# 1/rms of three images spread by rounded products, and the second gathers of the first chunk behind a clearing on GpSimd

## The chip, the core and the metric

The kernel runs on one core of a Trainium2 chip. A core has five engines with an instruction queue each: TensorE (PE; its weight loads are shown apart as PEld), VectorE (DVE), ScalarE (ACT), GpSimd (POOL) and SyncE (SP), which here issues most DMAs. The metric is the device time of one execution in microseconds; the kernel before takes 865.17 us (median of three runs, 863.83 to 868.22).

## The reference

The program computes an attention block with talking heads and hands its output to a gated feed-forward block.

```python
def _attn_ref(q, k, v, w_pre, w_post):          # batch 4, 12 heads, 448 tokens, head width 64
    scores = scale * np.matmul(q, k.transpose(0, 1, 3, 2))
    scores = np.einsum('bhij,hg->bgij', scores, w_pre)      # mixes the heads
    attn = np.exp(scores - np.max(scores, axis=-1, keepdims=True))
    attn = attn / (np.sum(attn, axis=-1, keepdims=True) + 1e-09)
    attn = np.einsum('bhij,hg->bgij', attn, w_post)         # mixes the heads again
    return np.matmul(attn, v)

def _moe_ref(x, w_gate, w_val, w_out, rms_g):   # 1792 tokens, 768 -> 1536 -> 768
    rms = np.sqrt(np.mean(x * x, axis=-1, keepdims=True) + 1e-06)
    xn = x / rms * rms_g
    g = xn @ w_gate
    silu = g * (1.0 / (1.0 + np.exp(-g)))
    return silu * (xn @ w_val) @ w_out
```

## The kernel before

The order of all work is written out by hand; nothing is scheduled. The program has two parts. "Image" means one of the four batch entries, with 448 tokens each.

**Part A, attention** (`part_a`, L417). The rows of the score matrices are cut into 16 chunks of up to 120, four an image, and each chunk into five or six steps. For each head pair a product q·k (`qk_mm`, L134) goes to PSUM; ACT and DVE copy it to a tile `st` (`qk_evac`, L146), and DMAs gather the rows of all heads into a tile `r` (L173), so that the heads of one row lie on neighbouring partitions. A step then mixes the heads (`premix`, tile `sp`, L182), takes the row maximum on DVE (L189) and the exponential on ACT (L196), scales the second mixing weights on POOL (L208), mixes again (`postmix`, tile `pm`, L223), and later multiplies by v (L267). Three tiles `r` take turns. They are cleared at the start, because the gathers leave some rows out: `r0` by DVE (L424), `r1` and `r2` by POOL (L425, L436).

For the first chunk each head's gather is in two: the columns of the first three steps at once (L173), the others put on a list `held` and issued after the last product of the chunk (L434). Of the 13 on the list five go to POOL's queue and eight to SP's. SP's gathers reuse eight completion semaphores in turn, with ACT's: a gather waits until the one that used the semaphore last has landed.

Beside this POOL adds the two halves of the attention output `xt` (L290), squares and sums them (L297 to L305), and SP stores them in DRAM.

**Part B, feed-forward** (`part_b`, L737). x is multiplied by the norm's weight and split into a rounded part and a rest (ACT L577, DVE L578), and each product is made of three rounded ones (L600 to L602, L608 to L610). The products of image 0 with the first weight column (`both`, called from `extra`) are laid between the last steps of part A. 1/rms of a token is put behind the product: it stands as a 112x4 tile `y` and has to be spread over all 128 partitions as `ry`. For that POOL makes a diagonal matrix times y (`diagonals`, tile `d`, L358; called in the last steps of part A, once for each of images 0 to 2), and PE multiplies it by a matrix of ones (`spread`, tile `psy`, L368). `first_row` (L791) begins with the spreads of images 0, 1 and 2, in this order, and then goes on with the products of images 1, 2 and 3. Image 3 comes later and has its diagonal made by DVE (`last_rms`, L827).

Engines take their instructions in order. So what stands behind a spread on PE waits until its diagonal is there.

Of the kernel before, what the change touches and what calls it, by code (L numbers as in the profile page):

```python
# [7 lines left out]
F32 = mybir.dt.float32  # L8
F32R = mybir.dt.float32r
# [3 lines left out]
ALU = mybir.AluOpType  # L13
# [3 lines left out]
B, H, S, D = 4, 12, 448, 64  # L17
# [21 lines left out]
JC, JP = 4, 112  # L39
# [6 lines left out]
def attention_moe(ctx: ExitStack, tc, q, k, v, wpre, wpost, mask, ident, wgv, wo, rms_g, out):  # L46
    nc = tc.nc
    NCHUNK = B * NC

    def pool(stack, name, bufs=1, **kw):  # L50
        return stack.enter_context(tc.tile_pool(name=name, bufs=bufs, reuse_waits="tile", **kw))
# [8 lines left out]
    ones = const.tile([128, 128], F32, name="ones")  # L60
# [31 lines left out]
    def setup():  # L92
        nc.vector.tensor_scalar(we, we, D ** -0.5, None, ALU.mult)
        nc.vector.memset(wk_pre, 0.0)
        for i, (o, w) in enumerate(((wk_pre[:, :HR], we), (wk, wp))):
            m = msk[:, i].unsqueeze(1).to_broadcast([128, H, RH])
            o = o.rearrange("p (h r) -> p h r", r=RH)
            nc.vector.tensor_tensor(o, w.unsqueeze(2).to_broadcast([128, H, RH]), m, ALU.mult)
# [7 lines left out]
    def load_q(n, hp, many=3, eng=nc.gpsimd):  # L106
        b, c = divmod(n, NC)
        if not hp:
            qt[n] = pq.tile([128, H // 2, 128], F32, name=f"q{n}", tag="q", bufs=2)
        hp = slice(hp, hp + many)  # L110
        eng.dma_start(qt[n][:, hp], q[b, :, c, hp])
# [9 lines left out]
    r_all = [(pr, pr, pq)[i].tile([128, 2 * KT, S], F32, name=f"r{i}", tag=f"r{i}", bufs=1) for i in range(3)]  # L121
# [160 lines left out]
    ry, sq, sums, xv, d = ({} for _ in range(5))  # L282
# [69 lines left out]
        ]  # L352
        return ops + 3 * step

    def diagonals(b, eng=nc.gpsimd):
        y = xv[b]
        d[b] = b_pools["dd" if b < B - 1 else "t2"].tile([128, S], F32, name="d", tag=f"d{b}" if b < B - 1 else "t", bufs=1 if b < B - 1 else 8)
        eng.tensor_tensor(  # L358
            d[b][:JP].rearrange("p (c i) -> p c i", c=JC),
            eye.unsqueeze(1).to_broadcast([JP, JC, JP]),  # L360
            y.unsqueeze(2).to_broadcast([JP, JC, JP]),
            ALU.mult,
        )

    def spread(b):

        ps = b_pools["ps0" if b == B - 1 else "ps_p"].tile([128, S], F32, name="psy", tag="p")
        nc.tensor.matmul(ps, ones[:JP], d.pop(b)[:JP], start=True, stop=True)  # L368
        ry[b] = (b_pools["wr"] if b == B - 1 else b_pools["t2"]).tile([128, S], F32, name=f"ry{b}", tag=f"ry{b}", bufs=1)
        nc.scalar.activation(ry[b], ps, AF.Copy)  # L370


    steps = [(n, p) for n in range(NCHUNK) for p in range(PAIRS[n % NC])]
    T = len(steps)
# [7 lines left out]
    for blk, ns in enumerate(BLOCKS):  # L382
        lo = first[ns[-1] + 1] + 1
        hi = first[ns[-1] + (3 if ns[-1] < 13 else 2)] + 1
        units = [(blk, i, part) for i in range(H // 2) for part in ((0, 1) if len(ns) > 1 else (None,))]
        for i, a in enumerate(units):
            t = lo + i * (hi - lo) // len(units)
# [7 lines left out]
    for n in range(NCHUNK):  # L395
        b, c = divmod(n, NC)
# [20 lines left out]
    def part_a(extra):  # L417
        for j in range(H // 4):
            load_q(0, 2 * j, 2, nc.scalar)
            load_k(0, 2 * j)  # L420
            load_k(0, 2 * j + 1)
        load_consts()
        load_q(1, 0, 6, nc.sync)
        nc.vector.memset(r_all[0], 0.0)  # L424
        nc.gpsimd.memset(r_all[1], 0.0)  # L425
        nc.vector.memset(ones, 1.0)
        for hp in range(H // 2):
            alone(qk_mm(0, hp))
            for j in range(2):
                qk_evac(0, hp, j)  # L430
            if hp == 4:
                setup()
        for i, args in enumerate(held):
            (nc.gpsimd if i % 5 in (1, 3) else nc.sync).dma_start(*args)  # L434
        load_q(2, 0)
        nc.gpsimd.memset(r_all[2], 0.0)  # L436
        load_q(2, 3)
        for hp in range(AHEAD):
            alone(qk_mm(1, hp))
            for j in range(2):  # L440
                qk_evac(1, hp, j)
        busy, = banks(ps_v, "busy", 1)
        for _ in range(4):
            nc.tensor.matmul(busy[:, :S], ones, kt[0, 0], start=True, stop=True)
        nc.sync.dma_start(g_sb, rms_g)
        nc.sync.dma_start(eye, ident)
        done = []
        for t in range(T + 24):
            def back(lag):
                return steps[t - lag] if 0 <= t - lag < T else None  # L450

            if t == first[NCHUNK - 1]:
                qk_ctx.close()
                start_b()
            for f, *a in jobs_at[t]:
                f(*a)
            while stored:
                x_store(*stored.pop(0))
            done = [(k, i // 2) for k, i, part in (av_at[t - 1] if t else []) if i % 2 and part != 0]
            sp = premix(*back(0)) if back(0) else []  # L460
            if qk_at[t]:
                qk = qk_mm(*qk_at[t][0])
                if any(f is sq_all and not a[1] for f, *a in last_at[t - 1]):
                    qk.reverse()
                order = sp[:1] + qk[1:] + sp[1:] + qk[:1]
            else:
                order = sp
            for x in order:
                for y in x:
                    y()  # L470
            for a in done:
                av_copy(*a)
            if back(0):
                rowmax(*back(0))
                expo(*back(0))
            if back(1):
                postmix(*back(1))
            for a in av_at[t]:
                av_mm(*a)
            for a in qk_at[t][:1]:  # L480
                for j in range(2):
                    qk_evac(*a, j)
            if back(1):
                for v_ in range(2):
                    evac_a(*back(1), v_)
            if back(0) and t >= T - 2:
                norm(*back(0))
            for op in sum_ops[: 1 if t < first[NCHUNK - 2] else 2 if t <= T else 4]:
                op()
                sum_ops.pop(0)  # L490
            if back(0) and t < T - 2:
                norm(*back(0))
            for a in qk_at[t][1:]:
                alone(qk_mm(*a))
                for j in range(2):
                    qk_evac(*a, j)
            for f, *a in last_at[t]:
                f(*a)
            for a in done:
                x_sum(*a)  # L500
            extra(t - T, bool(done))
            if t >= T + 4 and not done and not stored and not sum_ops and not any(av_at[t:]):
                break


    b_pools = {}
# [43 lines left out]
    def t_tile(name, tag="t", bufs=8):  # L550
        return b_pools["t2"].tile([128, S], F32, name=name, tag=tag, bufs=bufs)
# [117 lines left out]
    def start_b():  # L669
        b_pools["t2"] = pool(late, "t2", side="right")  # L670
        b_pools["x"] = pool(late, "xa", side="right")
        b_pools["w2a"] = pool(late, "w2a", side="right")
        b_pools["dd"] = pool(dd_ctx, "dd", side="right")
        b_pools["ps0"] = pool(late, "ps0", 2, space=PSUM, side="right")
        w[0] = [b_pools["w2a"].tile([128, FT, 128], F32R, name=f"w{n}", tag=f"w{n}") for n in "hl"]

        def w_load(p):
            raws["w", p] = t_tile("wf")[:, :384]
            nc.sync.dma_start(raws["w", p], wf[p // 2][:, (p % 2) * 384 : (p % 2) * 384 + 384])

        def w_split(p):
            hi, lo = (t[:, 3 * p : 3 * p + 3] for t in w[0])
            f = raws.pop(("w", p)).rearrange("p (a f) -> p a f", f=128)
            nc.scalar.activation(hi, f, AF.Copy)
            nc.gpsimd.tensor_tensor(lo, f, hi.bitcast(F32), ALU.subtract)

        def x_item(b, kk):
            todo.append([(x_load, b, kk), (x_split, b, kk, nc.vector), 0.7, 0, 0.9])

        for kk, p in ((0, 0), (None, 2), (1, 1), (None, 3)):  # L690
            if kk is not None:
                x_item(0, kk)
            todo.append([(w_load, p), (w_split, p), 0.5, 1.0, 0])
        for b in range(B - 1):
            for kk in range(0 if b else 2, KT):
                x_item(b, kk)
# [40 lines left out]
    def part_b(ps_p, raw_ctx):  # L737
# [83 lines left out]
        def last_rms(stage):  # L821
            if stage == 0:
                ps = b_pools["ps0"].tile([128, S], F32, name="pss", tag="p")
                column_sums(ps, 3)
                for op in rsqrt(ps[:JP, :JC], 3, const):
                    op()
                diagonals(3, nc.vector)  # L827
            else:
                spread(3)
                swiglu(3, 0, *first_ps[3])  # L830
# [164 lines left out]
```

## Time and profile before

| | |
|---|---|
| median of three runs | 865.17 us (863.83 to 868.22) |
| the profiled execution | 866.41 us, of which the profile's span is 864.6 us |
| PE busy | 827.3 us, 96% of the span |
| POOL busy | 437.6 us, 51% |
| DVE busy, ACT busy | 600.4 us, 69%; 390.4 us, 45% |
| chain that ended last, by engine | PE 90%, DMA 3%, issue 3%, POOL 2%, DVE 1% |

The chain is followed back from the last instruction, at each step to what released it. Part A ends at about 360 us of the span. Shares over the whole span say little of the two places that the change touches: the first 45 us, where gathers are late, and the stretch from 343 to 363 us, where part A passes into part B.

### The profile page before, as it was taken

To read this page: it belongs to the slowest core of one execution; us is meant where nothing else is said; L and a number is where in the kernel's file an instruction comes from. 1 tells how busy PE (TensorE), PEld (TensorE's weight loads), DVE (VectorE), ACT (ScalarE), POOL (GpSimd) and SP (SyncE) were. 2 spreads that over 40 slices of the span, in tenths; PEclk is the share of its full clock that TensorE was granted. 3 is DMA by queue.
4 is the path that set the end of the run, shared out by engine and by line. 5 is a ranking of instruction groups with operands and counts; after the bars stand their busy time and mean duration, and the time that the engine had idled before them with its cause. 6 is when DMAs were issued, how large, how long until landed. Compare 5 with 4: busy or idle time off the path is not lost.

```text
span 864.6 us, 26550 instructions
## 1 busy us (share of the span) xinstructions
PE 827.3 (96%) x10900; PEld 710.8 (82%) x10900; DVE 600.4 (69%) x985; ACT 390.4 (45%) x869; POOL 437.6 (51%) x537
## 2 busy tenths in 40 slices
PE   7899999998899898999999999999999999999998
PEld 2556777777678686799999999999999999999997
DVE  5676787887677666778655858576668359978461
ACT  3677777777677676732211222222121235554310
POOL 7233455554555347935634646365356369573100
PEclk9999999999999999999999999999999999999999
DMA  7777678667756653744634535535354246664541
GB/s 203 202 229 206 202 226 237 213 196 220 223 156 178 184 165 111 231 155 118 215 100 153 139 119 154 179 98 170 105 180 138 64 134 195 201 189 134 170 129 64
DMA packets 77547, 144.53 MB, mean 167 GB/s; under 512 B 10495, under 2 KB 66845, under 8 KB 77427
## 3 DMA queue, kind: packets, MB, share of 16 engines
q1 hardware_dynamic: 72814, 129.19, 49.0%
q0 software_dynamic: 3648, 11.31, 4.8%
q10 hardware_dynamic: 965, 2.34, 0.8%
q8 instruction: 86, 1.41, 0.7%
q14 instruction: 34, 0.28, 0.1%
HBM read 72.03 MB, written 31.21 MB: 119 GB/s over the span
## 4 chain that ended last, share of the span: by engine, by line
PE 90%; DMA 3%; issue 3%; POOL 2%; DVE 1%; ACT 0%; ACTq 0%; SPq 0%; POOLq 0%; DVEq 0%
PE pm L223 9%; PE qk L134 8%; PE sp L182 7%; PE av L267 7%; PE pg L608 6%; PE pg L609 6%; PE pv L609 6%; PE pg L610 6%; PE pv L610 6%; PE pv L608 6%; PE po L610 6%; PE po L609 6%; PE po L608 6%; DMA r<-st 3%; POOL d L358 0%
## 5 line engine op out<-in xcount | busy, mean ns | idle before, releaser
L182 PE MATMUL sp<-r,wk_pre 64*64 64x448 f32 x720 | 162.7, 539 | 4.4 <-DMA r<-st 2.0
L134 PE MATMUL qk<-k,q 64*64 64x448 f32 x768 | 154.6, 560 | 5.9 <-DMA q<-in_q 4.1
L196 ACT ACTIVATE e<-sp,nm 128x448 f32<-128x448 f32 x180 | 114.4, 638 | 88.4 <-DVE nm L189 86.2
L223 PEld LDWEIGHTS pm<-wn,e 60*64 60x64 f32 x5152 | 110.1, 134 | 50.9 <-POOL wn L208 21.5
L189 DVE TENSOR_REDUCE nm<-sp 128x1 f32<-128x448 f32 x180 | 111.5, 622 | 56.2 <-PE sp L182 25.3
L208 POOL TENSOR_SCALAR wn<-wk,rp 128x60 f32<-128x60 f32 x180 | 55.8, 322 | 162.4 <-DVE rp L205 143.1
L223 PE MATMUL pm<-wn,e 60*64 60x60 f32 x5152 | 109.5, 220 | 18.0 <-issue 14.9
L267 PE MATMUL av<-at_all,v 64*64 64x240 f32 (+4 forms) x1728 | 95.1, 319 | 3.6 <-issue 3.6
L608 PE MATMUL pg<-x,wh 128*128 128x448 f32 x264 | 96.8, 367 | 0.0
L609 PE MATMUL pv<-x,wh 128*128 128x448 f32 x264 | 96.4, 365 | 0.0
L608 PE MATMUL pv<-x,wh 128*128 128x448 f32 x264 | 96.4, 365 | 0.0
L610 PE MATMUL pg<-x,wl 128*128 128x448 f32 x264 | 96.4, 365 | 0.0
L610 PE MATMUL pv<-x,wl 128*128 128x448 f32 x264 | 96.4, 365 | 0.0
L609 PE MATMUL pg<-x,wh 128*128 128x448 f32 x264 | 96.4, 365 | 0.0
L595 DVE TENSOR_TENSOR x<-hraw,x 128x448 fp32r<-128x448 f32 x84 | 91.6, 1137 | 6.8 <-ACT x L594 6.8
L609 PE MATMUL po<-x,fac 128*128 128x448 f32 x252 | 92.1, 365 | 0.0
L608 PE MATMUL po<-x,fac 128*128 128x448 f32 x252 | 92.0, 365 | 0.0
L610 PE MATMUL po<-x,fac 128*128 128x448 f32 x252 | 92.0, 365 | 0.0
L642 POOL TENSOR_TENSOR sg<-sg,u 128x448 f32<-128x448 f32 x36 | 48.1, 1335 | 83.0 <-DVE u L638 43.5
L637 ACT ACTIVATE sg<-g 128x448 f32<-128x448 f32 x48 | 27.4, 571 | 129.2 <-DVE g L636 118.6
L182 PEld LDWEIGHTS sp<-r,wk_pre 64*64 64x64 f32 x720 | 62.4, 133 | 22.2 <-issue 9.6
L638 DVE TENSOR_TENSOR u<-pv,ry 128x448 f32<-128x448 f32 x48 | 29.9, 623 | 69.1 <-PE pv L610 60.6
(118 smaller groups left out, 1709.9 us busy)
## 6 DMA issues: line engine op xcount, KB each, us to landing
r<-st SPq DMA_DIRECT2D x117, 210.0 KB
hraw<-td SPq DMA_DIRECT2D x84, 224.0 KB
wraw<-in_wgv SPq DMA_DIRECT2D x20, 768.0 KB
td<-keep SPq DMA_DIRECT2D x48, 224.0 KB
wraw<-in_wo SPq DMA_DIRECT2D x12, 768.0 KB
r<-st SPq DMA_DIRECT2D x44, 175.0 KB
v<-in_v SPq DMA_DIRECT2D x24, 256.0 KB
q<-in_q POOLq DMA_DIRECT2D x28, 192.0 KB, 5.1
```

The costliest lines, as they stand in the source:

```text
L134: nc.tensor.matmul(ps[j][m, :S], qt[n][sl, hp, m], kt[n // NC, hp][sl], start=True, stop=True)
L182: nc.tensor.matmul(o, wk_pre[sl], rt[n][sl, 2 * p + v_], start=True, stop=True)
L189: nc.vector.tensor_reduce(t, ps[:, :S], AX.X, ALU.max, negate=True)
L196: nc.scalar.activation(e, ps[:, :S], AF.Exp, bias=nmx.pop((n, p, u)), accum_out=sm[n, p][:, u : u + 1])
L208: nc.gpsimd.tensor_scalar(wn[n, p][:, u], wk, r[:, u : u + 1], 1.0, ALU.mult, ALU.mult)
L223: nc.tensor.matmul(o[:, :, at_], e[u_][sl, j : j + JT], w_, start=True, stop=True)
L267: nc.tensor.matmul(x, vt[b, hp][sl, j, c_], a, start=(c_ == 0), stop=(c_ == JC - 1))
L595: nc.vector.tensor_tensor(lo, raw, hi.bitcast(F32), ALU.subtract)
L608: nc.tensor.matmul(ps, a, xh[:, kk], start=(kk == 0), stop=False)
L609: nc.tensor.matmul(ps, a, xl_[:, kk], start=False, stop=False)
L610: nc.tensor.matmul(ps, a2, xh[:, kk], start=False, stop=(kk == KT - 1))
L642: nc.gpsimd.tensor_tensor(h, sg, u, ALU.mult)
```

## The change

There are three edits.

1. For images 0 to 2, y is split into a rounded part `yh` (a copy on POOL that rounds) and the rest `yl` (a subtraction on POOL). POOL makes one diagonal of each (`dh`, `dl`), and PE makes `psy` of two rounded products, added in PSUM, in place of one plain fp32 product. A rounded copy of the matrix of ones is made once by DVE. Image 3 stays as it was.
2. In the first chunk POOL now loads q of chunk 2 and clears `r2` before it issues its five held gathers, not after. SP's eight stand where they stood.
3. `setup()` (five small DVE instructions that make the mixing weights) comes after the copies of head pair 5, not 4.

```diff
-    def diagonals(b, eng=nc.gpsimd):
-        y = xv[b]
-        d[b] = b_pools["dd" if b < B - 1 else "t2"].tile([128, S], F32, name="d", ...)
+    def diagonal(o, y, eng):
         eng.tensor_tensor(
-            d[b][:JP].rearrange("p (c i) -> p c i", c=JC),
+            o[:JP].rearrange("p (c i) -> p c i", c=JC),
             eye.unsqueeze(1).to_broadcast([JP, JC, JP]),
             y.unsqueeze(2).to_broadcast([JP, JC, JP]),
             ALU.mult,
         )
+    def diagonals(b):
+        y, p_ = xv[b], b_pools["dd"]
+        hi, lo = (p_.tile([JP, JC], F32R, name=f"y{n}{b}", tag=f"y{n}{b}") for n in "hl")
+        nc.gpsimd.tensor_copy(hi, y)
+        nc.gpsimd.tensor_tensor(lo, y, hi.bitcast(F32), ALU.subtract)
+        d[b] = []
+        for n, part in (("h", hi), ("l", lo)):
+            t = p_.tile([128, S], F32R, name=f"d{n}{b}", tag=f"d{n}{b}")
+            diagonal(t, part.bitcast(F32), nc.gpsimd)
+            d[b].append(t)
     def spread(b):
-        nc.tensor.matmul(ps, ones[:JP], d.pop(b)[:JP], start=True, stop=True)
+        if b == B - 1:
+            nc.tensor.matmul(ps, ones[:JP], d.pop(b)[:JP], start=True, stop=True)
+        else:
+            hi, lo = d.pop(b)
+            nc.tensor.matmul(ps, b_pools["ones"][:JP], hi[:JP], start=True, stop=False)
+            nc.tensor.matmul(ps, b_pools["ones"][:JP], lo[:JP], start=False, stop=True)
...
-            if hp == 4:
+            if hp == 5:
                 setup()
+        load_q(2, 0)
+        nc.gpsimd.memset(r_all[2], 0.0)
         for i, args in enumerate(held):
             (nc.gpsimd if i % 5 in (1, 3) else nc.sync).dma_start(*args)
-        load_q(2, 0)
-        nc.gpsimd.memset(r_all[2], 0.0)
         load_q(2, 3)
...
+        b_pools["ones"] = b_pools["dd"].tile([128, 128], F32R, name="ones_r", tag="ones_r")
+        nc.vector.tensor_copy(b_pools["ones"], ones)
```

On POOL, where part A passes into part B, before (y_5261 and y_6950 are the 1/rms of images 1 and 2; `d` are their diagonals):

```order
L290 TENSOR_TENSOR xt_7706<-xt_7706,xt_7707 128x200
L358 TENSOR_TENSOR d<-eye,y_5261 112x448
L297 TENSOR_TENSOR xt_7707<-xt_7706 128x200
L302 TENSOR_TENSOR sum_6957<-xt_7707 128x100
L290 TENSOR_TENSOR xt_7769<-xt_7769,xt_7770 128x200
L358 TENSOR_TENSOR d<-eye,y_6950 112x448
L297 TENSOR_TENSOR xt_7770<-xt_7769 128x200
```

The same place on POOL with the change:

```order
L290 TENSOR_TENSOR xt_7714<-xt_7714,xt_7715 128x200
L366 CAST yh_7774<-y_5261 112x4
L367 TENSOR_TENSOR yl_7775<-y_5261,yh_7774 112x4
L356 TENSOR_TENSOR dh_7778<-eye,yh_7774 112x448
L356 TENSOR_TENSOR dl_7780<-eye,yl_7775 112x448
L297 TENSOR_TENSOR xt_7715<-xt_7714 128x200
L302 TENSOR_TENSOR sum_6957<-xt_7715 128x100
L290 TENSOR_TENSOR xt_7783<-xt_7783,xt_7784 128x200
L366 CAST yh_7843<-y_6950 112x4
L367 TENSOR_TENSOR yl_7844<-y_6950,yh_7843 112x4
L356 TENSOR_TENSOR dh_7847<-eye,yh_7843 112x448
L356 TENSOR_TENSOR dl_7849<-eye,yl_7844 112x448
```

Each diagonal has become four instructions at the same place in the order; nothing else on POOL is moved there, and image 0 goes the same way.

On POOL at the start of the program, before (`r_119`, `r_120` and `r_121` are r0, r1 and r2; L434 are the held gathers, and the L173 behind them those of chunk 1):

```order
L173 DMA r_119<-st 10x6x448 x3
L434 DMA r_119<-st 10x6x448 x4
L434 DMA r_119<-st 5x6x448
L111 DMA q_238<-in_q 128x384
L436 MEMSET r_121 128x5376
L111 DMA q_238<-in_q 128x384
L173 DMA r_120<-st 10x12x448 x4
```

With the change:

```order
L173 DMA r_119<-st 10x6x448 x3
L111 DMA q_225<-in_q 128x384
L447 MEMSET r_121 128x5376
L449 DMA r_119<-st 10x6x448 x4
L449 DMA r_119<-st 5x6x448
L111 DMA q_225<-in_q 128x384
L173 DMA r_120<-st 10x12x448 x4
```

The five held gathers stand behind one load and the clearing; the rest of POOL's order is the same.

## Rows read from the trace of the kernel before

**Rows 1.** The page's first line.

```profile
span 864.6 us, 26550 instructions
```

**Rows 2.** Stretches of 362 to 860 us, summed: busy us of each engine.

```profile
sum 498.00, PE 497.99 PEld 460.80 DVE 337.61 ACT 142.71 POOL 247.76; mean PE 124.50 PEld 115.20 DVE 84.40 ACT 35.68 POOL 61.94
```

**Rows 3.** Chain that ended last, 343 to 363 us, shares of that stretch.

```profile
by line: POOL d L358 19.2%; POOL wl L685 17.2%; POOL xt L297 14.6%; POOL xt L290 14.3%; issue 11.3%; POOL sum L305 7.5%; POOL sum L302 5.5%; PE psy L368 5.1%; POOL xt L304 3.9%; POOL wn L208 1.6%; POOLq L290 0.3%; POOLq L685 0.2%
```

**Rows 4.** Timeline of POOL: start us, us, engine, line, operation, tiles, shapes, count.

```profile
357.21 1.31 POOL L358 TENSOR_TENSOR d<-eye,y 112x448 f32<-112x448 f32 x1
...
360.65 1.31 POOL L358 TENSOR_TENSOR d<-eye,y 112x448 f32<-112x448 f32 x1
361.92 0.90 POOL L297 TENSOR_TENSOR xt<-xt 128x200 f32<-128x200 f32 x1
```

**Rows 5.** Timeline of PE, 359.4 to 362.8 us; idle time before in brackets.

```profile
359.48 0.37 PE L602 MATMUL pv<-x,wl 128*128 128x448 f32 x1
359.69 1.67 PE L368 MATMUL psy<-d,ones 112*128 112x448 f32 x4
362.01 1.02 PE L368 MATMUL psy<-d,ones 112*128 112x448 f32 x2 [0.66 <-POOL d L358]
```

**Rows 6.** Waits of SP's queue, 0 to 60 us: total, times, longest.

```profile
SPq L173 <- DMA r<-st: 6.4, 4, 4.9
```

**Rows 7.** Timeline of ACT, 10 to 17 us.

```profile
10.74 1.71 ACTq L173 DMA_DIRECT2D r<-st  x1
...
13.07 0.78 ACTq L173 DMA_DIRECT2D r<-st  x1
```

**Rows 8.** Timeline of SP, from 12.7 us.

```profile
17.64 0.75 SPq L173 DMA_DIRECT2D r<-st  x1
```

**Rows 9.** Timeline of POOL, 7 to 26 us.

```profile
10.31 1.64 POOL L434 DMA_DIRECT2D r<-st  x3
13.33 1.10 POOL L434 DMA_DIRECT2D r<-st  x2 [1.37 <-ACT st L156]
...
15.14 4.60 POOL L436 MEMSET r<- 128x5376 f32 x1
```

**Rows 10.** Chain that ended last, 0 to 62 us, in order of time.

```profile
17.85 3.20 PE busy L444 x8
21.05 0.52 PE sp L182 x2
```

**Rows 11.** Waits, 18 to 62 us.

```profile
PE sp L182 <- DMA r<-st: 1.3, 3, 1.0
```

**Rows 12.** Timeline of POOL, small instructions that need one another.

```profile
327.60 0.20 POOL L346 TENSOR_TENSOR y<-u,y 112x4 f32<-112x4 f32 x1
327.88 0.20 POOL L343 TENSOR_TENSOR u<-y 112x4 f32<-112x4 f32 x1
```

**Rows 13.** Stretches: length, busy us (count) by engine, PEclk, DMA share, GB/s.

```profile
83.40:85.50 2.10, 0.00 (x0) 0.00 (x0) 0.92 (x2) 1.53 (x5) 0.48 (x1) 1.00 0.63 189
...
860.80:863.00 2.20, 0.00 (x0) 0.00 (x0) 0.62 (x1) 0.00 (x0) 0.00 (x0) 1.00 0.28 104
863.00:864.60 1.60, 0.00 (x0) 0.00 (x0) 0.00 (x0) 0.00 (x0) 0.00 (x0) 0.51 0.00 0
```

**Rows 14.** Timeline of PE's weight loads at the start, in groups of four.

```profile
4.12 0.31 PEld L134 LDWEIGHTS qk<-k,q 64*64 64x64 f32 x8 [4.12 <-DMA q<-in_q]
...
8.66 0.24 PEld L134 LDWEIGHTS qk<-k,q 64*64 64x64 f32 x4 [0.51 <-issue]
9.40 0.24 PEld L134 LDWEIGHTS qk<-k,q 64*64 64x64 f32 x4 [0.50 <-issue]
...
10.31 0.14 PEld L134 LDWEIGHTS qk<-k,q 64*64 64x64 f32 x4 [0.23 <-issue]
10.69 0.14 PEld L134 LDWEIGHTS qk<-k,q 64*64 64x64 f32 x4 [0.23 <-issue]
```

**Rows 15.** Timeline of DVE, last steps of part A.

```profile
327.67 1.16 DVE L189 TENSOR_REDUCE nm<-sp 128x1 f32<-128x448 f32 x2 [0.80 <-PE sp L182]
```

More of the change, by code (lines that the diff above doesn't have):

```diff
@@ L353, in rsqrt @@
         return ops + 3 * step
-    def diagonals(b, eng=nc.gpsimd):
-        y = xv[b]
-        d[b] = b_pools["dd" if b < B - 1 else "t2"].tile([128, S], F32, name="d", tag=f"d{b}" if b < B - 1 else "t", bufs=1 if b < B - 1 else 8)
+    def diagonal(o, y, eng):
         eng.tensor_tensor(
-            d[b][:JP].rearrange("p (c i) -> p c i", c=JC),
+            o[:JP].rearrange("p (c i) -> p c i", c=JC),
             eye.unsqueeze(1).to_broadcast([JP, JC, JP]),
@@ L363, in diagonals @@
         )
-    def spread(b):
-        ps = b_pools["ps0" if b == B - 1 else "ps_p"].tile([128, S], F32, name="psy", tag="p")
-        nc.tensor.matmul(ps, ones[:JP], d.pop(b)[:JP], start=True, stop=True)
+    def diagonals(b):
[8 more added lines that the diff above has]
+            d[b].append(t)
+    def spread(b):
+        if b == B - 1:
+            ps = b_pools["ps0"].tile([128, S], F32, name="psy", tag="p")
+            nc.tensor.matmul(ps, ones[:JP], d.pop(b)[:JP], start=True, stop=True)
+        else:
+            ps = b_pools["ps_p"].tile([128, S], F32, name="psy", tag="p")
+            hi, lo = d.pop(b)
+            nc.tensor.matmul(ps, b_pools["ones"][:JP], hi[:JP], start=True, stop=False)
+            nc.tensor.matmul(ps, b_pools["ones"][:JP], lo[:JP], start=False, stop=True)
         ry[b] = (b_pools["wr"] if b == B - 1 else b_pools["t2"]).tile([128, S], F32, name=f"ry{b}", tag=f"ry{b}", bufs=1)
@@ L826, in last_rms @@
                     op()
-                diagonals(3, nc.vector)
+                d[3] = t_tile("d")
+                diagonal(d[3], xv[3], nc.vector)
             else:
```

## The prediction, made before the result was known

> **What bounds the kernel now.** The page and the whole chain come first: the profiled execution took 866.4 us, its span is 864.6 [rows 1], PE carries nine tenths of the chain, so only what makes PE wait, or shortens PE's own work, can count. From 362 to 860 us PE is busy 497.99 of 498.00 us [rows 2]: part B has no slack that could take up a delay, and none that could hide one. What is lost before 362 stays lost.
>
> Second, the chain cut to the stretch where part A passes into part B. There POOL is the chain: its halves' sums, the weights' rests and the diagonals hold it, 19.2% the diagonals alone, PE only 5.1% [rows 3]. POOL's timeline shows it working without a pause; the last diagonal runs from 360.65 and the next instruction starts 1.27 us later [rows 4]. PE's timeline shows the other side: four passes of the first two spreads at 359.69, behind the last product of image 0, then 0.66 us of waiting for the last diagonal, and the third spread at 362.01 [rows 5]. So the end of POOL's last diagonal already sets when PE goes on.
>
> Third, the waits of the start. SP stood 4.9 us before the last gather of chunk 0, for the landing of a gather that ACT issued at 10.74 [rows 6, 7], and issued it at 17.64 [rows 8]. Its semaphore is shared with that one. Five held gathers of POOL are in flight just then (issued 10.31 to 14.4) [rows 9]. But PE hardly follows SP here: `sp` of step 0 starts at 21.05 right behind the filling products that begin at 17.85 [rows 10], and until 62 us PE waits for gathers 1.3 us in all [rows 11].
>
> **The diagonals and the spreads.** Each image gets three more POOL instructions: a copy and a subtraction on 112x4, and a second 112x448 product. Small dependent instructions on such tiles start 0.28 us apart (327.60, 327.88) [rows 12]; a diagonal holds POOL for 1.27 us (three alike, the last from 360.65 to 361.92) [rows 4]. That makes 0.28 + 0.28 + 1.27 = 1.83 us an image, and 5.49 for three, all ahead of or in the last one. POOL has no pause there, and nothing between them is dropped, so the third image's last diagonal is done 5.49 us later: PE's last product of the spreads starts at 362.01 + 5.49 = 367.50.
>
> PE saves little. An fp32 spread is two passes, at most 1.67 / 4 = 0.42 us each [rows 5]; rounded products of the same size start 0.21 apart (359.48 to 359.69) [rows 5]. Of the savings of images 0 and 1 nothing counts, as PE then waits for image 2. There 0.8 us follow the diagonal before; with the change the product of the rounded part runs while POOL makes the second diagonal, and 0.2 us follow. So the delay is 5.49 - 0.6 = 4.9 us. Bounds: POOL may run faster once DVE has no splits left, but hardly below the 0.90 us of a 200-wide product [rows 4], 3 x (0.56 + 0.90) - 0.6 = 3.8; and 5.5 if PE's saving does not come through. I take 4.9, since the three diagonals there are all alike.
>
> The rounding copy on POOL is in no row. From below it may be as cheap as the other small ones (0.20 busy), from above 1.3 us, a 448-wide product; I take 0.28, since what it moves is the same 112x4.
>
> **The clock.** With the change PE has, from 359.7 to 367.7, six products of 0.2 us and nothing else: image 1 is ready at about 358.5 + 2 x 1.83 = 362.1, the rounded part of image 2 at 366.2. So it idles 3.8 us in one piece with other idle time on both sides. [...] Coming back costs time: at the start PE worked from 4.12 on; its groups of four loads stood 0.74 us apart up to 9.40, and 0.38 from 10.31 on [rows 14]. About 5.6 us at half speed lose 2.8 us. I take 2.8, with 0 (the clock holds) as the other end.
>
> [...]
>
> **The start.** The five held gathers of POOL leave the time from 10.3 to 14.4. The load of q needs the first chunk's last product, done at about 11.5 (the twelfth group of four weight loads, at 10.69, belongs to it) [rows 14]; the clearing takes 4.6 us [rows 9], so they are issued from about 16.8 to 19.5, and what follows on POOL stands where it stood, since the same work is only turned round. Held gathers are used in step 3, some 10 us later. The gather that SP waited for shares the DMA engines with fewer others; half of the 4.9 us seems fair, so SP runs 2 to 2.5 us earlier. What PE can get of that is its wait for gathers, 1.3 us [rows 11], less what the five late ones cost again: I take -1.1. Bounds: -2.2, if ACT's issue at 10.74 also falls from 1.71 to 0.78 as the next one [rows 7] and the filling products start 0.9 earlier; +0.5, if the held gathers only crowd the next ones.
>
> **At nothing.** `setup()` moves 0.6 us of DVE work past one copy; nothing reads its tiles before 21.05, and ACT's queue, not DVE, holds the products of chunk 1. If that cover were gone it would cost 0.6. DVE's rounded copy of the ones comes ahead of a row maximum that waits 0.80 us for PE [rows 15], longer than such a copy of 128x128 can take; uncovered, 0.2.
>
> **The sum.** -1.1 + 4.9 + 2.8 = +6.6 us. The profiled execution would go from 866.4 to 873.0. It lies 1.2 us above the median of the runs, so for that I put 865.2 + 6.6 = 871.8.
>
> **Rivals.** *The clock holds.* For: two products of image 2 and the weight loads interrupt the idle time; the 2.1 us at 83.4 did no harm [rows 13]. Against: the end of the trace, where as little was enough. Then -1.1 + 4.9 = +3.8: 869.0.
>
> *The lead of SP is passed on in full, and it comes out not slower.* If the landing at which SP stands comes 4.9 us earlier [rows 6], and all of chunk 0 and 1 moves up with it, -4.9 + 4.9 = 0: 865.2, or 868.0 with the clock's 2.8. It decides from a lead of SP above 2.5 us if PE is bound by gathers. For it: SP issues gathers back to back after 17.64. Against: `sp` starts straight behind products that need no gather [rows 10], and the 1.3 us of waiting [rows 11].
>
> *The second diagonals are hidden.* If PE had something else to do ahead of the third spread, only savings would be left, -1.1 - 0.6 = -1.7: 863.5, faster by 0.2%. Against: the spreads stand in front of all products of image 1, in order, and PE waits there already [rows 5].
>
> *The first rounding copy is slow.* It is a kind of instruction that POOL runs nowhere before. If its first one took as long as a whole diagonal more [rows 4], 1.3 us, the sum is +7.9: 873.1. [...]
>
> **How the numbers follow.** Forecast 0.70 (871.8; its own range 869.5 to 874), clock holds 0.14 (869.0), lead passed on 0.07 (865 to 868), diagonals hidden 0.03 (863.5), slow copy 0.06 (873.1). Runs of this kernel differ by 2 us or so from their median, and about 0.5%, 4.3 us, is what can be told from no change; 869.5 is the border. Slower: 0.70 x 0.9 + 0.14 x 0.4 + 0.06 = 0.75. Faster: a half of the 0.03, and a little of the lead's case: 0.02. Same: 0.23. The range has to hold both clocks and the bounds of the start and of the diagonals; it leaves out most of the two cases below 867: 867.0 to 874.5.
>
> **What would show it.** Right: waits of PE for `dh` and `dl` of some 5 us together between 361 and 367, POOL without a pause up to there, the last `psy` at about 366.4 (367.5 less the start's 1.1), and a dip of the granted clock behind it. Wrong: no wait for the last diagonal; a full clock throughout; an `sp` of step 0 well before 20 us, which would make the start worth more than 1.1; a rounding copy of more than 1 us.

## The result

The changed kernel takes 874.11 us (median of six runs, 870.85 to 876.51), the kernel before 865.04 beside it. The ratio is 1.0117, 95% interval [1.0082, 1.0152], slower by 7 to 13 us. The forecast was 871.8 with a range up to 874.5. On the forecast's own base of 865.17 the ratio gives 875.3: slower as forecast, but by 10.1 us instead of 6.6 and beyond the range. Measured twice more, the changed kernel gave 1.0122 [1.0073, 1.0172] and 1.0088 [1.0053, 1.0123].

The profiled execution took 873.61 us, 7.2 more than that of before. First the transition from part A to part B. POOL's timeline there (start us, us, engine, line, operation, tiles, shapes; image 1, then image 2):

```profile
360.17 0.19 POOL L366 CAST yh<-y 112x4 fp32r<-112x4 f32 x1
360.44 0.53 POOL L367 TENSOR_TENSOR yl<-y,yh 112x4 fp32r<-112x4 f32 x1
360.93 1.37 POOL L356 TENSOR_TENSOR dh<-eye,yh 112x448 fp32r<-112x448 f32 x1
362.26 0.93 POOL L356 TENSOR_TENSOR dl<-eye,yl 112x448 fp32r<-112x448 f32 x1
...
364.65 0.60 POOL L366 CAST yh<-y 112x4 fp32r<-112x4 f32 x1
365.33 0.53 POOL L367 TENSOR_TENSOR yl<-y,yh 112x4 fp32r<-112x4 f32 x1
365.82 1.37 POOL L356 TENSOR_TENSOR dh<-eye,yh 112x448 fp32r<-112x448 f32 x1
367.16 0.93 POOL L356 TENSOR_TENSOR dl<-eye,yl 112x448 fp32r<-112x448 f32 x1
368.05 0.51 POOL L297 TENSOR_TENSOR xt<-xt 128x200 f32<-128x200 f32 x1
```

It answers to [rows 4]. From the copy to the instruction behind the last diagonal POOL now spends 2.99 and 3.40 us where one diagonal took 1.27; the instruction behind image 2's starts at 368.05 and not at 361.92, 6.13 later. PE's timeline, which answers to [rows 5], with the idle time before an instruction in brackets:

```profile
360.10 0.37 PE L381 MATMUL psy<-dh,ones_r 112*128 112x448 f32 x1
360.30 0.37 PE L382 MATMUL psy<-dl,ones_r 112*128 112x448 f32 x1
362.36 0.47 PE L381 MATMUL psy<-dh,ones_r 112*128 112x448 f32 x1 [1.69 <-POOL dh L356]
363.25 0.47 PE L382 MATMUL psy<-dl,ones_r 112*128 112x448 f32 x1 [0.43 <-POOL dl L356]
367.25 0.74 PE L381 MATMUL psy<-dh,ones_r 112*128 112x448 f32 x1 [3.52 <-POOL dh L356]
368.14 0.74 PE L382 MATMUL psy<-dl,ones_r 112*128 112x448 f32 x1
368.68 0.57 PE L613 MATMUL pg<-x,wh 128*128 128x448 f32 x1
369.05 0.57 PE L614 MATMUL pg<-x,wh 128*128 128x448 f32 x1
```

PE waits 5.6 us for diagonals instead of 0.66, and then its products start 0.37 us apart instead of 0.20. Stretches of the same trace (length, PE busy, granted clock, share of the DMA engines, GB/s) show why: behind the wait the clock stands at 0.50 for 2.6 us of work, and then at 1.00:

```profile
368.70:371.30 2.60, 2.60 (x9) 0.50 0.86 347
371.40:372.40 1.00, 1.00 (x7) 1.00 0.08 23
```

Second the start. The chain that ended last, 10 to 35 us, in order of time, which answers to [rows 10]:

```profile
12.17 4.93 DVE we L93
...
22.26 0.52 PE sp L182 x2
...
24.42 9.29 DMA r<-st
...
33.96 1.01 PE sp L182 x2
```

And the three timelines behind it: SP's last gather of chunk 0 and its held ones (the second fence has the held ones before), POOL's clearing, and DVE's `setup()` (its first instruction before in the fence behind it).

```profile
14.79 0.75 SPq L173 DMA_DIRECT2D r<-st  x1
15.64 10.86 SPq L449 DMA_DIRECT2D r<-st  x8
```

```profile
18.49 8.68 SPq L434 DMA_DIRECT2D r<-st  x8
```

```profile
12.47 4.60 POOL L447 MEMSET r<- 128x5376 f32 x1
16.99 2.77 POOL L449 DMA_DIRECT2D r<-st  x5
```

```profile
12.17 4.93 DVE L93 TENSOR_SCALAR we<-we 128x12 f32<-128x12 f32 x1
17.41 1.15 DVE L154 COPY st<-qk 128x448 f32<-128x448 f32 x2
```

```profile
11.50 0.16 DVE L93 TENSOR_SCALAR we<-we 128x12 f32<-128x12 f32 x1
```

SP issues the last gather of chunk 0 at 14.79 instead of 17.64 [rows 8], as it waits 2.4 us there and not 4.9 [rows 6]. But its eight held gathers then take 10.86 us and not 8.68, so that of the 2.85 us some 0.7 are left at their end. And `setup()`'s first instruction, of 12 columns, takes 4.93 us (0.16 before) and ends with POOL's clearing. The copies of q·k behind it are late, and `sp` of step 0 starts at 22.26, not 21.05. Then PE stands 3.11 us in step 3 for a held gather [rows 11: 1.3 us in all], and the clock falls there too (0.50 from 33.42 to 36.83). The first product of part B starts at 347.46, before at 347.02; as the repeats below show, these two executions alone can't tell what the start costs.

### The profile page after: what moved, and what is told of

The parts are those of the page before. It is cut to its first block, busy times and chain, and to the rows that moved or that the text cites. A ratio compares the mean times of both kernels' runs of the same rounds, so it can differ in the third digit from the quotient of the medians.

```text
span 871.8 us, 26564 instructions
## 1 busy us (share of the span) xinstructions
PE 830.7 (95%) x10900; PEld 711.2 (82%) x10900; DVE 602.2 (69%) x986; ACT 390.0 (45%) x869; POOL 442.0 (51%) x546
## 4 chain that ended last, share of the span: by engine, by line
PE 90%; POOL 3%; issue 3%; DMA 2%; DVE 2%; ACT 0%; SPq 0%; POOLq 0%; DVEq 0%; ACTq 0%
PE pm L223 9%; PE qk L134 8%; PE sp L182 8%; PE av L267 7%; PE pg L621 6%; PE pv L621 6%; PE pg L623 6%; PE pv L623 6%; PE pg L622 6%; PE pv L622 6%; PE po L622 6%; PE po L623 6%; PE po L621 6%; DMA r<-st 2%; DVE we L93 1%
## 5 line engine op out<-in xcount | busy, mean ns | idle before, releaser
L223 PE MATMUL pm<-wn,e 60*64 60x60 f32 x5152 | 107.7, 219 | 13.2 <-issue 9.8
```

The source lines that it names most:

```text
L223: nc.tensor.matmul(o[:, :, at_], e[u_][sl, j : j + JT], w_, start=True, stop=True)
```

## The experiments

Executions of one kernel differ by 1.5 to 4.3 us (standard deviation), mostly in part A: with both moves of the start alone the first pv below lies between 342.85 and 352.35 us, the stretch behind it between 53.30 and 53.66. The granted clock of part A differs too; in the three profiles of the changed kernel it is 0.97, 0.92 and 0.97 in the mean of 10 to 62 us. So beside the ratios I read one stretch that holds the transition and nothing of part A: from PE's first product `pv` of part B to the spread of image 3. In the kernel before and the changed kernel it runs between these rows of PE's timeline, 53.14 and 59.75 us:

```profile
347.02 0.36 PE L600 MATMUL pv<-x,wh 128*128 128x448 f32 x1
400.16 0.92 PE L368 MATMUL psy<-d,ones 112*128 112x448 f32 x2
```

```profile
347.46 0.37 PE L613 MATMUL pv<-x,wh 128*128 128x448 f32 x1
407.21 0.92 PE L377 MATMUL psy<-d,ones 112*128 112x448 f32 x2
```

| kernel | ratio to before, 95% interval | first pv, us | stretch, us |
|---|---|---|---|
| before, unchanged, as an experiment | 0.9986 [0.9956, 1.0017] | 348.70 | 53.52 |
| changed, again | 1.0122 and 1.0088 | 351.62, 348.26 | 60.42, 59.65 |
| spreads alone, twice | 1.0083 [1.0047, 1.0119], 1.0113 [1.0068, 1.0158] | 342.55, 346.43 | 60.97, 60.69 |
| both moves of the start alone, three times | 1.0016 [0.9976, 1.0056], 1.0082 [1.0045, 1.0120], 1.0029 [0.9995, 1.0063] | 352.35, 342.85, 348.24 | 53.66, 53.30, 53.63 |
| held gathers alone, twice | 1.0017 [0.9973, 1.0062], 1.0084 [1.0048, 1.0120] | 345.35, 351.48 | 53.79, 53.26 |
| `setup()` alone | 1.0061 [1.0030, 1.0092] | not read | not read |
| changed, `setup()` back | 1.0115 [1.0074, 1.0156] | 347.76 | 59.99 |
| changed, held gathers back | 1.0066 [1.0037, 1.0096] | 343.86 | 60.53 |
| start's moves, clearing cut | 1.0005 [0.9976, 1.0034] | 347.95 | 53.80 |
| spreads alone, waits filled | 1.0040 [1.0012, 1.0069] | 344.51 | 58.17 |
| spreads alone, without the rest | 1.0012 [0.9979, 1.0045] | 343.26 | 55.52 |
| spreads alone, late, twice | 1.0017 [0.9982, 1.0051], 1.0093 [1.0058, 1.0129] | 345.75, 347.54 | 55.95, 55.18 |

### The spreads alone

The kernel before with edit 1 only.

> The rounded spreads alone, the start as before. Theory A (the transition makes nearly all of the loss: POOL's three extra instructions an image, about 5.7 us as the changed kernel's trace has them, and the clock's fall behind them, about 1.5 us, less PE's saving): the kernel is 6 to 7 us longer than before (871 to 872 us, ratio 1.007 to 1.008); the trace shows POOL's last diagonal ending near 367.6, PE waiting for dh of images 1 and 2, and one fall of the granted clock behind it and none near 33 us. Theory B (the start makes the 2 to 3 us by which the medians lie further apart than the two profiled executions do): +6 or less here, and the rest in the run with the start alone. If instead this run alone gives the whole +9 to +10, theory B is wrong and the transition or the clock costs more in other executions than in the profiled one.

It gave 1.0083, theory A's size, and a second time 1.0113. The waits are those of the changed kernel (what waited for what: total, times, longest), and the clock stays at 0.50 for longer, to 368.9:

```profile
PE psy L381 <- POOL dh L356: 5.1, 2, 3.6
```

```profile
363.80:368.80 5.00, 5.00 (x15) 0.50 0.48 188
369.00:370.00 1.00, 1.00 (x7) 1.00 0.91 186
```

One expectation missed: with the start as before the granted clock is 0.97 in the mean of 10 to 62 us, where the profile of before has 1.00. A fall in part A is thus no sign of the start's moves.

> The spreads alone once more (start as before), beside the changed kernel: 1.007 to 1.009 if the start makes the difference of 3 us between the two, 1.010 to 1.012 if the difference so far was chance. From the first pv to PE's last spread of image 3 about 61 us, as the first time (53.5 before).

The repeat, beside the changed kernel (1.0088), came out above it at 1.0113: the 3 us between the two in the first batches were at least partly chance.

### Without the rest

```diff
-        hi, lo = (p_.tile(...) for n in "hl")
-        nc.gpsimd.tensor_tensor(lo, y, hi.bitcast(F32), ALU.subtract)
-        for n, part in (("h", hi), ("l", lo)):
+        hi = p_.tile(...)
+        for n, part in (("h", hi),):
```

> The spreads alone (start as before), with the rounded part only: the rest, its diagonal and its product are left out, so the rows of 1/rms are rounded. POOL then adds only the copy (0.2 to 0.6 us an image in the trace of the spreads alone). If POOL's length ahead of the third spread is what costs, the end of the last diagonal moves by 0.6 to 1.8 us instead of 5.7, PE's wait for it goes from 3.6 to about 1 us, the clock holds, and the stretch from the first pv to the end is 518 to 519.5 us: +0 to +1.5 us over before, 6 to 7 us less than the spreads alone. If the form of the spread (fp32r operands, the new evictions) costs, it stays at 522 or more.

Ratio 1.0012; the stretch is 55.52, 4.8 less than the mean of the seven profiles with the whole edit (60.29). POOL's length is what costs, not the form of the product. The copy took 0.18 to 0.59 us. Wrong was that the clock would hold: PE still waits 3.1 us for one diagonal, and behind it the clock reads 0.50 for 3.3 us (360.7 to 364.0); so the stretch is 2.0 us above the old spreads, and not 0 to 1.5.

```profile
PE psy L380 <- POOL dh L356: 3.1, 1, 3.1
```

### Waits filled

```diff
+            idle = ps_p.tile([128, S], F32, name="idle", tag="p")
+            for b, many in enumerate((0, 8, 15)):
+                for _ in range(many):
+                    nc.tensor.matmul(idle, w[0][0][:, 0], xs[1][0][:, 0], start=True, stop=True)
                 spread(b)
```

> The spreads alone (start as before), and PE fills its waits ahead of the second and third spread with 8 and 15 products of 128x448 into a tile that nothing reads, so that it doesn't stand still. POOL's diagonals take as long as in the spreads alone. Theory (the idle time lets the clock fall, and that costs 1.5 us in the changed kernel and about 3 in the run with the spreads alone): no fall of the granted clock within 10 us of the spreads, products of image 1 at 0.20 us from the first on, and the stretch from the first pv to the end 521.5 to 523 us instead of 525.4. Rival (a clock that falls anyway, or products that delay the spread by as much as the fall costs): 525 or more.

PE's timeline has the fillers in the waits, and the first product of image 1 is followed by the next after 0.21 us:

```profile
357.59 1.81 PE L813 MATMUL idle<-x,wh 128*128 128x448 f32 x8
359.33 0.48 PE L381 MATMUL psy<-dh,ones_r 112*128 112x448 f32 x1
360.23 0.47 PE L382 MATMUL psy<-dl,ones_r 112*128 112x448 f32 x1 [0.41 <-POOL dl L356]
360.53 3.21 PE L813 MATMUL idle<-x,wh 128*128 128x448 f32 x15
363.79 0.47 PE L381 MATMUL psy<-dh,ones_r 112*128 112x448 f32 x1
365.06 0.47 PE L382 MATMUL psy<-dl,ones_r 112*128 112x448 f32 x1 [0.81 <-POOL dl L356]
365.38 0.37 PE L613 MATMUL pg<-x,wh 128*128 128x448 f32 x1
365.59 0.37 PE L614 MATMUL pg<-x,wh 128*128 128x448 f32 x1
```

The clock keeps 1.00 (362 to 368 us), and the stretch is 58.17: 2.1 less than with the spreads as they are, 4.7 more than the mean of eight profiles with the old spreads (53.51). That separates the transition's loss of 6.8 us into 4.7 for POOL and 2.1 for the clock, by one profile with fillers; the seven without lie between 59.65 and 60.97. To the end of the span the stretch did not shrink as expected (525.3 us), because here the last part, from image 3's spread on, took 467.1 us instead of 464.5. The three profiles of the start alone have the same 2.6 us, no other profile has. In the first of them 70 us of the output stage hold 341 products of PE, in the kernel before 347, at a granted clock of 1.00 in both. What makes it is not known; the time of those two kernels contains it.

### Late spreads

```diff
-            for b in range(B - 1):
-                spread(b)
...
+            spread(0)
+            more()
             for kk in range(KT):
                 both(first_ps[1], w[0], xs[1], kk)
+            spread(1)
+            spread(2)
...
```

> The rounded spreads, but those of images 1 and 2 are issued behind the first product group of image 1 instead of ahead of it; the start as before. Theory A says the extra POOL work costs only because the spreads stand ahead of all products of image 1, so that PE waits for the last diagonal: here PE has those products to do, the waits for dh and dl go to nearly 0, the clock does not fall, and the time is that of before or 1 to 2 us less (ratio 0.998 to 1.000). Rival: the evictions of the first products need the spread rows of image 1 (ry) and wait for POOL's diagonal instead, so that PE stalls on full product tiles a few us later: then +2 to +4 us.

Here `both` is the first product group of image 1, and `more()` only takes its PSUM tiles. The waits for diagonals are gone, and others have come in their place: PE reaches a later part of x before ACT and DVE have split it.

```profile
PE pg L613 <- ACT x L590: 1.2, 1, 1.2
PE pg L614 <- DVE x L591: 1.1, 1, 1.1
```

The stretch is 55.95, 2.4 above the old spreads: between theory A and the rival, whose price was right but not its cause.

> The rounded spreads with those of images 1 and 2 behind the first products of image 1, again: the first time it took 0.5 us less than before in the mean (standard error 1.2), though in its profile image 1's next split was late by 2.35 us and the stretch from the first pv to image 3's spread 2.8 us longer. If the order alone made the transition's loss, 0.998 to 1.001; if the split is late in every execution, 1.002 to 1.004.

The second profile has 55.18 with the same two waits (0.9 and 1.3 us). Its ratio of 1.0093 can't be read as the order's, as the section on the start shows. So of the transition's 6.8 us some 4.7, by the mean of these two profiles, lay in the order: a diagonal is dear only where PE has nothing else to do.

### The start's two moves

> The start's two moves alone (held gathers behind the clearing, setup() behind pair 5), the spreads as before. What the changed kernel's trace shows should be here again: setup()'s first DVE instruction takes about as long as POOL's clearing (4.9 us, 0.16 before), `sp` of step 0 starts about 1.2 us later, PE waits about 3 us in step 3, and the granted clock falls there. Theory A (most of that is given back before the transition, 0.4 us left): +0.3 to +1 us, ratio 1.000 to 1.001. Theory B (the start's loss and its falls of the clock vary from one execution to the next, and cost 2 to 4 us in the median): ratio 1.003 to 1.005, with a lower mean granted clock than before in each run. The prediction's own term would be -1.1 us.

> The start's two moves alone, again. If the start costs 2 to 3 us: ratio 1.002 to 1.004, and the first pv at 348 to 352 us in the profile (342.6 to 347.0 with the old start). If it costs nothing in the mean: 0.998 to 1.001, and the first pv among those of the old start. The hold of DVE (4.9 us) and `sp` of step 0 at 22 or later are expected either way.

> The start's two moves alone, a third time (1.0016 and 1.0082 so far). Against the unchanged kernel of the same batch: if the start costs 2 to 3 us in every batch, 0.2 to 0.4% above it; if it costs nothing in the mean, within 0.2% of it.

In all six profiles with both moves (three here, three of the changed kernel) `setup()`'s first instruction takes 4.93 us and `sp` of step 0 starts at 22.2 to 23.4 (20.3 to 22.2 in the eight profiles with the start as before). The wait in step 3 is not always there: PE waited for gathers 0 to 4.3 us between 18 and 62 us, with the old start 0 to 4.5.

### Held gathers alone, and the clearing cut

> The held gathers behind the clearing, setup() where it was (behind pair 4). If setup()'s long DVE instruction comes from running beside POOL's clearing, it is short here (0.16 us, at about 11.5, ahead of the clearing) and `sp` of step 0 starts at about 21 or, if SP's earlier first gathers are worth something, at 20 to 20.5. If the wait of 3 us in step 3 comes from the held gathers alone, it is still there (2.5 to 3.5 us, as PE arrives 1.2 us earlier: up to 4.3) and the clock falls there as well; the time is then within 1 us of the run that has both moves. If the wait came from the delay of the DVE copies, it is gone and the time is that of before or 1 us less.

DVE's `setup()`, PE's first `sp`, and the waits of 18 to 45 us:

```profile
10.55 0.16 DVE L93 TENSOR_SCALAR we<-we 128x12 f32<-128x12 f32 x1
```

```profile
19.66 0.59 PE L182 MATMUL sp<-r,wk_pre 64*64 64x448 f32 x2
```

```profile
PE sp L182 <- DMA r<-st: 4.5, 2, 4.1
```

Ahead of the clearing the instruction is short, and step 0 starts some 1.3 us earlier than in the profile before, 0.7 earlier than in the earliest with the old start. In step 3 PE waits 4.1 us.

> The held gathers behind the clearing alone, again: no hold of DVE, `sp` of step 0 at 19.5 to 21, a wait of 3 to 4 us in step 3 with a fall of the clock. If what SP wins is lost again in step 3, the ratio is 0.999 to 1.002; if the prediction's -1.1 us is to be had once setup() is out of the way, 0.997 to 0.999.

The repeat has no hold either, but `sp` at 21.09, and 6.2 us of waiting for gathers: the gain isn't there each time, the wait was both times.

> The start's two moves as in the changed kernel, spreads as before, but POOL's clearing of the target is cut into 12 memsets of 448 columns each. If setup()'s first DVE instruction can't start or end while one POOL instruction runs, it takes one piece's time here (0.4 to 0.8 us, not 4.9), the DVE copies behind it start at about 13, and `sp` of step 0 starts at 19.5 to 21 instead of 22.2. If DVE is held until POOL leaves the whole row of memsets, it stays at 4.9 and 22.2. The wait in step 3 for a held gather stays in either case (3 to 4 us). Time: within 2 us of before.

The edit, and DVE's and POOL's rows:

```diff
+            for i in range(2 * KT):
+                nc.gpsimd.memset(r_all[2][:, i], 0.0)
-        nc.gpsimd.memset(r_all[2], 0.0)
```

```profile
11.79 0.30 DVE L93 TENSOR_SCALAR we<-we 128x12 f32<-128x12 f32 x1
...
12.13 0.22 DVE L98 TENSOR_TENSOR wk_pre<-we,msk 128x60 f32<-128x60 f32 x1
```

```profile
12.10 5.03 POOL L435 MEMSET r<- 128x448 f32 x12
```

The clearing takes 5.03 us, longer than the 4.60 of the whole one, yet the instruction takes 0.30, and `sp` starts at 20.12. It is recorded 0.3 us ahead of POOL's clearing, as in the changed kernel (12.17 and 12.47), so what holds DVE is the one long POOL instruction; that a piece holds it for its own length isn't shown, as here it ends when the first piece starts. In this run PE waits 5.5 us in step 3, more than in any other.

### Back to before, one move at a time

> The changed kernel itself, once more, beside the experiments of this batch, as executions of one kernel differ by several us here (the start of the run with the spreads alone is that of before, and yet its first product of part B comes 4.5 us earlier). If the loss is the transition's (6.8 and 7.8 us from the first product pv of part B to the end of the span, in the changed kernel and in the run with the spreads alone) plus a start worth 0 to 1, the ratio comes out at 1.008 to 1.010; if the start really costs 2 to 3 us more, at 1.011 to 1.013. In its profile the stretch from the first pv to the end is 524 to 525.5 us (517.6 before), setup()'s first DVE instruction takes 4.9 us again, and PE waits 3 to 4 us for a held gather in step 3.

> The changed kernel, with setup() behind pair 4 again, ahead of the clearing, as in the kernel before. The changed kernel took 1.0117 and 1.0122 of before's time, the spreads alone 1.0083: 3 us more, which only the start can make. Theory L (DVE held by the clearing makes it: step 0 starts 1 to 2.5 us late in the three profiles that have the hold, and PE stands still while the copies are late): setup()'s first instruction takes 0.16 us, `sp` of step 0 starts at 19.5 to 20.5 (22.2 and 23.4 in the changed kernel), and the ratio is 1.008, as with the spreads alone. Theory H (the held gathers, issued late and landing up to 12 us after their issue, make it): PE waits 3 to 5 us in step 3 as in the run with the held gathers moved alone (4.15), and the ratio stays at 1.011 to 1.012.

> The changed kernel, with the held gathers ahead of the clearing again, and setup() behind pair 5. The clearing then starts at about 15, behind setup() (about 12.2), so the hold of DVE should be gone too (0.16 us), and SP stands for the landing of ACT's gather again (`sp` of step 0 at about 21). Theories L and H both expect the ratio of the spreads alone, 1.008. If it stays at 1.011 or more, the 3 us aren't from the start's held gathers at all, but from chance or the later place of setup().

> The changed kernel, for comparison on the same chip as the two runs above and the one below: ratio 1.010 to 1.013 if the two measurements so far hold; step 0 at 22 to 23.5.

With `setup()` back the hold is gone (0.16 us), PE waits 3.6 us in step 3, and the ratio stays at 1.0115, as theory H had it. `sp` starts at 21.12, later than theory L expected. With the held gathers back the ratio is 1.0066, and the first pv comes at 343.86. But the intervals, [1.0074, 1.0156] and [1.0037, 1.0096], overlap, and the spreads alone, with neither move, had 1.0113 beside them: the ratios don't tell the two moves apart.

A mark nearer to the start does. PE's first product with v (tile `av`) starts, in the kernel before, the changed kernel, the held gathers back and the clearing cut, at:

```profile
67.17 0.37 PE L267 MATMUL av<-at_all,v 64*64 64x240 f32 x1
```

```profile
68.92 0.37 PE L267 MATMUL av<-at_all,v 64*64 64x240 f32 x1
```

```profile
67.38 0.37 PE L267 MATMUL av<-at_all,v 64*64 64x240 f32 x1
```

```profile
70.29 0.37 PE L267 MATMUL av<-at_all,v 64*64 64x240 f32 x1
```

In the eight profiles with the start as before it lies between 65.34 and 68.45 (mean 66.8), in the six with both moves between 68.06 and 70.47 (69.3), in the three with the held gathers alone moved between 69.10 and 69.75 (69.4). So the start costs some 2.5 us by then, with a standard error of 0.5. It comes with the held gathers. Taking DVE's hold away, in two ways, gave nothing of it back, and with `setup()` moved alone, in one profile, the product lies among those of the old start.

> setup() behind pair 5 alone, the held gathers ahead of the clearing as before: the clearing starts at about 15, so DVE isn't held (0.16 us), `sp` of step 0 at about 21 as before, and the ratio is that of no change, 0.998 to 1.002. If setup()'s place costs by itself (its 0.6 us ahead of the copies), `sp` comes 0.5 us later.

It missed: 1.0061, where no change was expected. Its profile can't be compared with the others, so what its `setup()` took isn't known; 0.16 us is what it takes at the same place with the held gathers back.

> The kernel before, unchanged, measured like an experiment. If the comparisons are even: ratio 0.998 to 1.002. If a part of the last batch's differences belongs to how the executions of a batch follow one another: 1.003 or more, and then that much has to be allowed for in each of the comparisons here, the changed kernel's too.

In the batch of `setup()` alone, of the second runs of the start's moves, of the held gathers and of the late spreads, all four lay 0.6 to 0.9% above before, and three of them had lain 0.2% above it in an earlier batch. The unchanged kernel shows no such offset in its own batch (0.9986). In that batch it was also the kernel before that ran shorter, 862.6 us in the median against 865.0 to 867.5 in the others. What made the batch differ is open. Between batches a difference under some 0.6% can't be put down to an edit, and the start's cost can't be had from the times more finely than this: 1.4 to 7 us, by the batch, with the 2.6 us of the last part in it. Nor do the ratios of the changed kernel (1.0117, 1.0122, 1.0088) and of the spreads alone (1.0083, 1.0113) show it. The first pv, mean of six profiles with both moves, is 348.5 us, of eight with the start as before 345.7, of the three with the held gathers alone moved 348.2: 2.5 to 2.8 us later, with a scatter of 2 to 3.5 us in each group and so a standard error of some 1.6. That agrees with the 2.5 us at the first `av`, which is the firmer figure.

## Why the prediction fell short

**The diagonals, +4.9.** Right in its mechanism; the size came out by errors that cancel. 5.49 us were forecast for POOL; the last diagonal is done 5.7 us later once the start's 0.44 is taken off. The small instructions were dearer than 0.28 (0.27 to 0.68 from one to the next), the second diagonals cheaper than 1.27 (0.90). PE's waits were to be some 5 us: 5.6. The net cost with the clock held is 4.7. The first rounding copy isn't slow: 0.58 us, so that rival is out.

**The clock, +2.8.** Right that it falls: behind the wait it reads 0.50 for 2.6 us of work in the changed kernel and for 5.0 in the spreads alone, and 1.00 with the waits filled; the five other profiles with the same spreads have stretches as long (59.65 to 60.69 us, filled 58.17). That 3.8 us of idling would be enough was the author's estimate. The runs have a clock at 0.50 behind waits of 3.52 us (changed), 3.6 (spreads alone) and 3.1 (without the rest), and still at 1.00 in the changed kernel's wait of 1.69. The fall cost 2.1 us in the mean (the fillers), 0.7 less than forecast, between about 1.6 in the changed kernel and 2.8 in the spreads alone: over the last wait the clock reads 0.62 in the one and 0.50 in the other, and PE has less or more work at 0.50.

**The start, -1.1.** This is the step that failed. It had three premises.

*SP's lead of 2 to 2.5 us, half of the 4.9 us that SP stood.* It came, 2.85 us, but the 4.9 us were those of one execution: the kernel before, unchanged, issued the same gather at 15.05 in another, with `sp` of step 0 at 20.34.

```profile
15.05 0.75 SPq L173 DMA_DIRECT2D r<-st  x1
```

And SP's list of held gathers used most of the lead up: the eight ended 0.7 us earlier than before.

*Held gathers used late enough ("some 10 us later").* They weren't: the one that PE waited for in step 3 was issued at 24.42 and landed 9.29 us later, and with the held gathers behind the clearing PE waits 2.7 to 5.5 us in step 3 in the four profiles without the hold of DVE, 0 to 3.1 in the six with it, where it comes later; with the old start 0 to 2.3 us. Why the landing takes so long isn't shown. Two of SP's held issues took 1.86 and 3.42 us where the other six take 0.75 to 1.12; but before two took 1.95 and 1.69, and with the held gathers back one took 3.09, so this isn't peculiar to the new order.

*`setup()` moved "at nothing" past one copy, "0.6 if the cover were gone".* In fact it was moved beside the clearing, which the other edit had brought forward from 15.14 to 12.47, and there one of its instructions held DVE for 4.93 us. Step 0 then starts later; but as PE waits less in step 3, the first `av` comes no later with the hold (69.3 in the mean) than without it (69.4, and 70.29 with the clearing cut), so the profiles show no price of the hold by itself.

In place of -1.1 the profiles have +2.5 up to the first `av`, more than the term's bound of +0.5. With 4.7 and 2.1 that makes 9.3 us, against 1.0088 to 1.0122 of 865, 7.6 to 10.6.

Not every DVE instruction beside such a clearing is held. In the kernel before it ran from 15.14 to 19.74 us, and the copies from PSUM beside it took 0.62 us, as the one ahead of it:

```profile
14.16 0.62 DVE L154 COPY st<-qk 128x448 f32<-128x448 f32 x1 [0.33 <-PE qk L134]
15.57 0.62 DVE L154 COPY st<-qk 128x448 f32<-128x448 f32 x1 [0.78 <-PE qk L134]
17.94 0.62 DVE L154 COPY st<-qk 128x448 f32<-128x448 f32 x1 [1.75 <-PE qk L134]
```

A TENSOR_TENSOR of `setup()` took 0.22 us beside a piece of the cut clearing (12.13), and 0.22 in the changed kernel behind the whole one (17.14). The TENSOR_SCALAR that was held there is recorded 0.30 us ahead of the clearing. Which DVE instructions a clearing holds, and why, isn't shown.

The rivals: the clock didn't hold, the second diagonals weren't hidden, and SP's lead of 2.85 us, above the 2.5 that this rival asked for, wasn't passed on.

## What to carry to other kernels

Where the strictly ordered main engine waits for a helper engine at a barrier, as here, most of what the helper gets longer is lost (4.7 us of 5.7), and the clock's fall behind the wait comes on top (2.1). Look first for work that can stand ahead of the barrier: issuing two of the three spreads one product group later gave back some two thirds of the loss, until the next supply was late. When two edits each look free, lay their new times side by side: what had been apart (a small DVE instruction and a long clearing) may now run at the same time. A wait read from one execution is one draw: before a gain is taken from it, look at it in a second. To price an edit near the start, read a mark near the start; 280 us later the scatter had grown to the size of the effect. And before a loss under 1% is put down to an edit, run the kernel in a second batch.

## What was not expected of the hardware

One GpSimd memset of 128x5376 held a DVE instruction of 12 columns for 4.93 us, in each of the six profiles where the two met; with the same clearing cut into twelve it took 0.30 in the one profile. And in two programs, one of them profiled three times, the part from image 3's spread on took 467.0 to 467.1 us, where the others have 464.4 to 464.6; where its products were counted, 70 us hold 341 instead of 347, at a granted clock of 1.00.
